# Two 128-unit chunks per turn of the first matmul, in the order whole, tiled, tiled, whole

## The chip, the cores and the metric

The kernel runs on one core of one Trainium2 chip. The time is that of the device, in microseconds (us), from one launch. Three runs of the kernel before gave 829.6, 832.7 and 833.99 us, median 832.7 us. The profile comes from one more execution, of 831.74 us. Its span, from the first to the last recorded event, is 829.9 us. Engines are named as in the profile: PE is TensorE running matmuls, PEld is TensorE loading weights, DVE is VectorE, ACT is ScalarE, POOL is GpSimd and SP is SyncE.

## The reference

A short causal convolution over tokens is followed by a two-layer network with a gated activation. Eight sequences of 4096 tokens have 192 channels each; the hidden layer has 2048 units.

```python
# convolution: 7 taps, softmax-normalised weights, one set for each of 8 heads of 24 channels
w = softmax(weight, axis=-1)                   # (8, 7)
conv[b, s, h, g] = sum_k w[h, k] * x_pad[b, s + k, h, g]
# network, on 8 * 4096 = 32768 tokens of 192 channels
h = conv @ w_in                                # (32768, 192) @ (192, 2048)
g = h * (1.0 / (1.0 + np.exp(-beta * h)))
out = g @ w_out                                # (32768, 2048) @ (2048, 192)
```

## The kernel before

The work is cut into 32 stages (`N_ST`). One stage holds 512 tokens (`TOK`) of each of two sequences, called halves `h` here; so a stage has 1024 tokens. Channels lie on the partitions. Channels 0 to 127 of both halves stand in `ct[:, 0, :]` and `ct[:, 1, :]`. The other 64 channels of the two halves share one slice: `ct[0:64, 2, :]` belongs to half 0 and `ct[64:128, 2, :]` to half 1. The weights `w_in_s` have the same split: `[:, 0, :]` for the first 128 channels and `[:, 1, :]` for the last 64, held twice, on rows 0 to 63 and again on rows 64 to 127.

**First matmul (`hidden`).** The 2048 hidden units are cut into 16 chunks (`NF`) of 128. For each chunk there are four matmuls of 512 columns into a tile `ph` of two PSUM banks, one bank for each half. Two take the first 128 channels, and so all 128 rows of the array (line 218, called *whole* below, W). Two take the last 64 channels, one on rows 0 to 63 and the other on rows 64 to 127 (line 221, called *tiled*, T). Then ScalarE applies the activation from `ph` into `g` (line 224). Each matmul has its own weight load. There are three `ph` buffers.

**Second matmul (`output`).** For each block of 128 tokens, sixteen matmuls add up over the hidden units, with `g` as the weights and 192 columns of `w_out_s` (line 239, called O below). A part is half a block, eight matmuls. Every fourth part is followed by a VectorE copy of `po` (line 247), and every eighth part by a store from SyncE's queue.

**Order.** The schedule is written by hand and each engine runs its instructions in program order. In the main loop a stage has 16 turns `u`. In turn `u` the kernel issues chunk `u` of the first matmul of stage `s`, part `u` of the second matmul of stage `s - 1`, and one VectorE operation of the convolution of stage `s + 1` (14 in all, lines 195, 197 and 206). Stage 0 has no second matmul. Its VectorE also scales the weights: `prep_w_in` (line 170) ahead of turns 0, 4, 8 and 12, and `prep_w_out` (line 177) in every turn. After stage 31 a last pass has only the 16 parts of the second matmul.

On TensorE a turn of stages 1 to 31 is therefore: two W, two T, eight O.

Of the kernel before, what the change touches and what calls it, by code (L numbers as in the profile page):

```python
# [8 lines left out]
FP32 = mybir.dt.float32  # L9
BF16 = mybir.dt.bfloat16  # L10
AF = mybir.ActivationFunctionType
# [4 lines left out]
def kernel(  # L16
# [15 lines left out]
    nc = tc.nc  # L32
# [6 lines left out]
    DB = D - DA  # L39
    TOK = 512  # L40
# [4 lines left out]
    N_ST = (B // 2) * CHUNKS  # L45
# [18 lines left out]
    psum_h = ctx.enter_context(  # L64
        tc.tile_pool(name="psum_h", bufs=3, space=bass.MemoryType.PSUM)
    )
# [9 lines left out]
    def cast(s):  # L76
        p, c = divmod(s, CHUNKS)
        r0 = HALO if c == 0 else 0
        t0 = c * TOK - HALO + r0
        t1 = (c + 1) * TOK  # L80
        xd = xd_pool.tile([HALO + TOK, 3, DA], BF16, name="xd")
        nc.gpsimd.dma_start(out=xd[r0:, 0:2, :], in_=x_v[p, t0:t1, :, 0:DA])  # L82
        nc.gpsimd.dma_start(  # L83
            out=xd[r0:, 2, :].rearrange("t (h d) -> t h d", h=2),
            in_=x_v[p, t0:t1, :, DA:D],
        )
        xds[s] = xd

    def xpose(s):
        r0 = HALO if s % CHUNKS == 0 else 0  # L90
        xd = xds.pop(s)
        xt = xt_pool.tile([128, 3, HALO + TOK], BF16, name="xt")
        if r0:
            nc.vector.memset(xt[:, :, 0:HALO], 0.0)
        nc.sync.dma_start_transpose(  # L95
            xt[:, :, r0:], xd[r0:, :, :].rearrange("t c d -> t (c d)")
        )
        xts[s] = xt
# [61 lines left out]
    beta = consts.tile([128, NF], FP32)  # L160
# [4 lines left out]
    w_in_s = consts.tile([128, 2, F], BF16)  # L165

    def prep_w_in(i):
        cols = slice(i * FW, (i + 1) * FW)
        for j in range(2):
            nc.vector.tensor_scalar_mul(  # L170
                w_in_s[:, j, cols], w_in_raw[i][:, j, :], w_last[:, j : j + 1]
            )
# [3 lines left out]
    def prep_w_out(c):  # L176
        nc.vector.tensor_scalar_mul(  # L177
            w_out_s[:, c, :], w_out_raw[:, c, :], beta_r[:, c : c + 1]
        )
# [4 lines left out]
    def conv_ops(s):  # L184
        xt = xts.pop(s)
        ct = ct_pool.tile([128, 3, TOK], BF16, name="ct")
        cts[s] = ct
        ops = []
        for j, cs in ((0, slice(0, 2)), (1, slice(2, 3))):

            def tap(k, j=j, cs=cs):
                src = xt[:, cs, HALO - PAD + k : HALO - PAD + k + TOK]
                dst = ct[:, cs, :]
                if k == 0:
                    nc.vector.tensor_scalar_mul(dst, src, cw[:, j, 0:1])  # L195
                elif k < K - 1:
                    nc.vector.scalar_tensor_tensor(  # L197
                        out=dst,
                        in0=src,
                        scalar=cw[:, j, k : k + 1],  # L200
                        in1=dst,
                        op0=ALU.mult,
                        op1=ALU.add,
                    )
                else:
                    nc.vector.tensor_tensor(dst, src, dst, ALU.add)  # L206

            ops += [lambda k=k, tap=tap: tap(k) for k in range(K)]
        return ops

    gs = {}

    def hidden(s, fc):
        ct, g = cts[s], gs[s]
        ph = psum_h.tile([128, 2, TOK], FP32, name="ph")
        w = w_in_s[:, :, fc * 128 : (fc + 1) * 128]
        for h in range(2):
            nc.tensor.matmul(ph[:, h, :], w[:, 0, :], ct[:, h, :], start=True, stop=False)  # L218
        for h in range(2):
            rows = slice(h * DB, (h + 1) * DB)  # L220
            nc.tensor.matmul(  # L221
                ph[:, h, :], w[rows, 1, :], ct[rows, 2, :], start=False, stop=True
            )
        nc.scalar.activation(g[:, fc, :, :], ph, AF.Silu, scale=beta[:, fc : fc + 1])  # L224

    pos, osbs = {}, {}

    def output(s, part):

        blk, half = divmod(part, 2)  # L230
        h, q = divmod(blk, N_BLK)
        g = gs[s]
        if part % 4 == 0:
            pos[s] = psum_o.tile([128, 2, D], FP32, name="po")
        if part % 8 == 0:
            osbs[s] = osb_pool.tile([128, N_BLK, D], FP32, name="osb")
        po, osb = pos[s], osbs[s]
        for fc in range(half * NF // 2, (half + 1) * NF // 2):
            nc.tensor.matmul(  # L239
                po[:, q % 2, :],  # L240
                g[:, fc, h, q * BLK : (q + 1) * BLK],
                w_out_s[:, fc, :],
                start=(fc == 0),
                stop=(fc == NF - 1),
            )
        if part % 4 == 3:
            nc.vector.tensor_copy(osb[:, q - 1 : q + 1, :], po)  # L247
        if part % 8 == 7:
            p, c = divmod(s, CHUNKS)
            nc.sync.dma_start(out=out_v[h, p, c], in_=osb)  # L250
# [4 lines left out]
    for s in range(N_ST + 1):  # L255
        if s < N_ST:
            gs[s] = g_pool.tile([128, NF, 2, TOK], BF16, name="g")
        ops = conv_ops(s + 1) if s + 1 < N_ST else []
        for u in range(NF):
            if s == 0 and u % (NF // NW) == 0:  # L260
                prep_w_in(u // (NF // NW))
            if s < N_ST:
                hidden(s, u)
            if s > 0:
                output(s - 1, u)
            if u < len(ops):
                ops[u]()
            if s == 0:
                prep_w_out(u)
            if u == 0 and s + 3 < N_ST:  # L270
                cast(s + 3)
            if u == 1 and s + 2 < N_ST:
                xpose(s + 2)
# [30 lines left out]
```

## Time and profile before

| what | us |
|---|---|
| three runs, median (lowest, highest) | 832.7 (829.6, 833.99) |
| the profiled execution, its own time | 831.74 |
| its span | 829.9 |
| PE busy | 784.3 |
| PEld busy | 445.7 |
| ACT busy | 572.7 |
| DVE busy | 462.8 |
| from the first O (61.67) to the last turn's O (814.07) | 752.40 |

Times in the span count from its start. A row of the timeline has the start, the length, the engine, the line, the operation, the output and inputs and how many instructions were merged; a square bracket at the end holds the idle time of the engine ahead of it and what ended it. Matmuls are pipelined and the end of one is modelled: two that overlap in the rows run one behind the other on the array. So matmuls are compared by their starts, not by their lengths.

### The profile page before, as it was taken

What the parts mean: (1) busy time and instruction counts of PE and PEld (TensorE: products, weight loads), DVE (VectorE), ACT (ScalarE), POOL (GpSimd) and SP (SyncE); (2) the same over time, 40 slices, a digit from 0 to 9 for tenths busy, and PEclk for the clock granted to TensorE, in tenths of its full rate; (3) what the DMA queues carried; (4) which work ended last, traced back from release to release, by engine and by line L of the source; (5) the groups of instructions that cost most, each with busy time, mean ns of one, the idle gap of its engine ahead of it and who ended that gap; (6) DMA issues with size and microseconds to landing.
All of it is one profiled execution on the core that took longest, in us unless ns stands there. A gap on an engine that the chain in (4) does not pass through costs nothing.

```text
span 829.9 us, 13854 instructions
## 1 busy us (share of the span) xinstructions
PE 784.3 (95%) x6145; PEld 445.7 (54%) x6145; DVE 462.8 (56%) x613; ACT 572.7 (69%) x516; POOL 82.5 (10%) x70
## 2 busy tenths in 40 slices
PE   0279999999999999999999999999999999999997
PEld 0015555555555555555555555555555555555556
DVE  2696665555656556565555656555565665555601
ACT  1267777777777777777777777777777777777772
POOL 8389800000000000000000000000000000000000
PEclk9989999999999999999999999999999999999999
DMA  9999991210322221122222112222201322220111
GB/s 143 222 169 179 182 120 41 58 53 25 59 58 46 53 58 43 35 59 58 39 58 59 36 42 59 58 39 58 59 28 51 59 59 39 58 54 25 39 39 59
DMA packets 157341, 55.60 MB, mean 67 GB/s; under 512 B 121425, under 2 KB 156257, under 8 KB 157281
## 3 DMA queue, kind: packets, MB, share of 16 engines
q1 hardware_dynamic: 88592, 41.77, 22.1%
q0 software_dynamic: 68352, 12.93, 18.9%
q8 instruction: 48, 0.79, 0.4%
q10 hardware_dynamic: 337, 0.02, 0.0%
q14 instruction: 12, 0.10, 0.0%
HBM read 29.54 MB, written 38.09 MB: 81 GB/s over the span
## 4 chain that ended last, share of the span: by engine, by line
PE 93%; DMA 4%; DVE 2%; SPq 1%; issue 0%; POOL 0%; POOLq 0%
PE po L239 47%; PE ph L218 26%; PE ph L221 20%; DMA xt<-xd 2%; DMA w_in_raw_107<-in_moe_w_in_dram 1%; DVE ct L197 1%; DMA xd<-in_x_dram 1%; DVE w_out_s L177 1%; DVE w_in_s L170 0%; SPq L95 0%; SPq L133 0%; SPq L131 0%; DVE ct L195 0%; DVE ct L206 0%; SPq L136 0%
## 5 line engine op out<-in xcount | busy, mean ns | idle before, releaser
L224 ACT ACTIVATE g<-ph,beta 128x1024 bf16<-128x1024 f32 x512 | 569.6, 1114 | 233.6 <-PE ph L221 233.6
L239 PE MATMUL po<-w_out_s,g 128*128 128x192 bf16 x4096 | 424.0, 247 | 0.0
L239 PEld LDWEIGHTS <-g 128*128 128x128 bf16 x4096 | 312.4, 98 | 112.2 <-issue 112.2
L218 PE MATMUL ph<-ct,w_in_s 128*128 128x512 bf16 x1024 | 308.2, 383 | 31.1 <-DVE w_in_s L170 31.1
L197 DVE SCALAR_TENSOR_TENSOR ct<-xt,cw,ct 128x1024 bf16<-128x1024 bf16 (+1 forms) x320 | 325.1, 1016 | 8.8
L247 DVE COPY osb<-po 128x384 f32<-128x384 f32 x128 | 71.4, 557 | 329.0 <-PE po L239 329.0
L221 PE MATMUL ph<-ct,w_in_s 64*128 64x512 bf16 x1024 | 201.7, 391 | 0.8 <-DVE w_in_s L170 0.8
L221 PEld LDWEIGHTS <-w_in_s 64*128 64x128 bf16 x1024 | 49.3, 93 | 221.3 <-issue 217.8
L218 PEld LDWEIGHTS <-w_in_s 128*128 128x128 bf16 x1024 | 91.3, 98 | 36.8 <-DVE w_in_s L170 32.3
L82 POOL DMA_DIRECT2D xd<-in_x_dram x32 | 42.6, 1330 | 12.4 <-DMA xd<-in_x_dram 11.6
L83 POOL DMA_DIRECT2D xd<-in_x_dram x32 | 42.5, 1327 | 8.3 <-DMA xd<-in_x_dram 7.9
L206 DVE TENSOR_TENSOR ct<-xt,ct 128x1024 bf16<-128x1024 bf16 x64 | 35.7, 557 | 2.1
L195 DVE TENSOR_SCALAR ct<-xt,cw 128x1024 bf16<-128x1024 bf16 x64 | 27.6, 431 | 14.1 <-DMA xt<-xd 13.3
L177 DVE TENSOR_SCALAR w_out_s<-w_out_raw,beta_r 128x192 bf16<-128x192 f32 x16 | 8.9, 568 | 0.0
L159 PE MATMUL po<-ident,beta_q 16*128 16x16 f32 x1 | 0.3, 254 | 9.2 <-DMA beta_q<-in_moe_beta_dram 9.2
L146 ACT ACT_TABLE_LOAD x1 | 1.3, 1283 | 6.1 <-DMA cw<-in_weight_dram 6.1
L159 PEld LDWEIGHTS po<-ident,beta_q 16*128 16x128 f32 x1 | 0.2, 176 | 9.1 <-issue 9.1
L144 DVE TENSOR_REDUCE nmax<-cw 128x2 f32<-128x14 f32 x1 | 0.2, 168 | 7.7 <-DMA cw<-in_weight_dram 7.7
L224 ACT ACT_TABLE_LOAD x1 | 1.3, 1283 | 1.5 <-DVE beta L161 1.5
L170 DVE TENSOR_SCALAR w_in_s<-w_in_raw_115,w_last 128x512 bf16<-128x512 f32 x2 | 1.5, 800 | 0.0
L146 ACT ACTIVATE cw<-cw,nmax 128x7 f32<-128x7 f32 x2 | 0.5, 294 | 1.4 <-DVE nmax L144 1.4
L170 DVE TENSOR_SCALAR w_in_s<-w_in_raw_111,w_last 128x512 bf16<-128x512 f32 x2 | 1.5, 774 | 0.0
(16 smaller groups left out, 4.7 us busy)
## 6 DMA issues: line engine op xcount, KB each, us to landing
out_dram<-osb SPq DMA_DIRECT2D x64, 384.0 KB, 3.0
xd<-in_x_dram POOLq DMA_DIRECT2D x28, 264.0 KB, 10.1
xd<-in_x_dram POOLq DMA_DIRECT2D x28, 132.0 KB, 10.2
w_out_raw<-in_moe_w_out_dram SPq DMA_DIRECT2D x1, 1536.0 KB, 12.8
xd<-in_x_dram POOLq DMA_DIRECT2D x4, 256.0 KB, 9.1
xd<-in_x_dram POOLq DMA_DIRECT2D x4, 128.0 KB, 8.7
xt<-xd SPq DMA_TRANSPOSE x32, 4.6
w_in_raw_103<-in_moe_w_in_dram SPq DMA_DIRECT2D x1, 256.0 KB
```

Source lines behind the costliest of these rows:

```text
L82: nc.gpsimd.dma_start(out=xd[r0:, 0:2, :], in_=x_v[p, t0:t1, :, 0:DA])
L83: nc.gpsimd.dma_start(out=xd[r0:, 2, :].rearrange("t (h d) -> t h d", h=2), in_=x_v[p, t0:t1, :, DA:D],)
L170: nc.vector.tensor_scalar_mul(w_in_s[:, j, cols], w_in_raw[i][:, j, :], w_last[:, j : j + 1])
L177: nc.vector.tensor_scalar_mul(w_out_s[:, c, :], w_out_raw[:, c, :], beta_r[:, c : c + 1])
L195: nc.vector.tensor_scalar_mul(dst, src, cw[:, j, 0:1])
L197: nc.vector.scalar_tensor_tensor(out=dst, in0=src, scalar=cw[:, j, k : k + 1], in1=dst, op0=ALU.mult, op1=ALU.add,)
L206: nc.vector.tensor_tensor(dst, src, dst, ALU.add)
L218: nc.tensor.matmul(ph[:, h, :], w[:, 0, :], ct[:, h, :], start=True, stop=False)
L221: nc.tensor.matmul(ph[:, h, :], w[rows, 1, :], ct[rows, 2, :], start=False, stop=True)
L224: nc.scalar.activation(g[:, fc, :, :], ph, AF.Silu, scale=beta[:, fc : fc + 1])
L239: nc.tensor.matmul(po[:, q % 2, :], g[:, fc, h, q * BLK : (q + 1) * BLK], w_out_s[:, fc, :], start=(fc == 0), stop=(fc == NF - 1),)
L247: nc.vector.tensor_copy(osb[:, q - 1 : q + 1, :], po)
```

## The change

`hidden` now takes two chunks at once and is called in every second turn `u`. Two `ph` tiles are taken together. The eight matmuls of the two chunks stand in the order W W of the first chunk, T T of the first, T T of the second, W W of the second. In the second chunk the tiled matmuls now start the accumulation and the whole ones end it. The two activations follow. Everything else in the loop stays, so the outputs of parts `u` and `u + 1`, sixteen matmuls, now stand one behind the other on TensorE, and a *turn* of the changed kernel is: two W, two T, two T, two W, sixteen O. The numbers of matmuls, weight loads and activations are the same.

```diff
-    def hidden(s, fc):
+    def hidden(s, fc0):
         ct, g = cts[s], gs[s]
-        ph = psum_h.tile([128, 2, TOK], FP32, name="ph")
-        w = w_in_s[:, :, fc * 128 : (fc + 1) * 128]
-        for h in range(2):
-            nc.tensor.matmul(ph[:, h, :], w[:, 0, :], ct[:, h, :], start=True, stop=False)
-        for h in range(2):
-            rows = slice(h * DB, (h + 1) * DB)
-            nc.tensor.matmul(
-                ph[:, h, :], w[rows, 1, :], ct[rows, 2, :], start=False, stop=True
-            )
-        nc.scalar.activation(g[:, fc, :, :], ph, AF.Silu, scale=beta[:, fc : fc + 1])
+        phs = [psum_h.tile([128, 2, TOK], FP32, name="ph") for _ in range(2)]
+        ws = [w_in_s[:, :, f * 128 : (f + 1) * 128] for f in (fc0, fc0 + 1)]
+
+        def whole(i, start):
+            for h in range(2):
+                nc.tensor.matmul(
+                    phs[i][:, h, :], ws[i][:, 0, :], ct[:, h, :], start=start, stop=not start
+                )
+
+        def tiled(i, start):
+            for h in range(2):
+                rows = slice(h * DB, (h + 1) * DB)
+                nc.tensor.matmul(
+                    phs[i][:, h, :], ws[i][rows, 1, :], ct[rows, 2, :], start=start, stop=not start
+                )
+
+        whole(0, True)
+        tiled(0, False)
+        tiled(1, True)
+        whole(1, False)
+        for i in range(2):
+            fc = fc0 + i
+            nc.scalar.activation(
+                g[:, fc, :, :], phs[i], AF.Silu, scale=beta[:, fc : fc + 1]
+            )
...
-            if s < N_ST:
+            if s < N_ST and u % 2 == 0:
                 hidden(s, u)
```

Before, TensorE's queue in the middle of a stage has, for one chunk (`ph_1017`), W, W, T, T, and then the outputs. Each row names the line, the instruction, and its output and inputs with their buffer numbers; LDWEIGHTS is the weight load ahead of each matmul. L218 is W, L221 is T, L239 is O.

```order
L218 LDWEIGHTS w_in_s_149
L218 MATMUL ph_1017<-ct_565,w_in_s_149 128x512 [waits Activation_49]
L218 LDWEIGHTS w_in_s_149
L218 MATMUL ph_1017<-ct_565,w_in_s_149 128x512
L221 LDWEIGHTS w_in_s_149
L221 MATMUL ph_1017<-ct_565,w_in_s_149 128x512
L221 LDWEIGHTS w_in_s_149
L221 MATMUL ph_1017<-ct_565,w_in_s_149 128x512
L239 LDWEIGHTS g_564
L239 MATMUL po_1023<-w_out_s_150,g_564 128x192 [waits DVE_49]
```

The outputs stand right behind the two T, and the only wait for ScalarE in the chunk is at its first W. In the changed kernel, at the same place of TensorE's queue, L221 is W and L228 is T (the line numbers have moved); `ph_1017` is the first chunk of the turn and `ph_1018` the second.

```order
L228 LDWEIGHTS w_in_s_149
L228 MATMUL ph_1017<-ct_565,w_in_s_149 128x512
L228 LDWEIGHTS w_in_s_149
L228 MATMUL ph_1017<-ct_565,w_in_s_149 128x512
L228 LDWEIGHTS w_in_s_149
L228 MATMUL ph_1018<-ct_565,w_in_s_149 128x512 [waits Activation_49]
L228 LDWEIGHTS w_in_s_149
L228 MATMUL ph_1018<-ct_565,w_in_s_149 128x512
L221 LDWEIGHTS w_in_s_149
L221 MATMUL ph_1018<-ct_565,w_in_s_149 128x512
```

Four T now stand together, the second chunk's W follow them, and there is a second wait for ScalarE, in the middle of the turn, at the second chunk's first T. The end of the turn on the same engine, where L255 is O:

```order
L221 LDWEIGHTS w_in_s_149
L221 MATMUL ph_1018<-ct_565,w_in_s_149 128x512
L255 LDWEIGHTS g_564
L255 MATMUL po_1029<-w_out_s_150,g_564 128x192 [waits DVE_49]
L255 LDWEIGHTS g_564
L255 MATMUL po_1029<-w_out_s_150,g_564 128x192
```

The outputs now follow a W, not a T.

## The prediction

> **What bounds the kernel.** I read the page's busy shares first, then the chain of work that ended last, then the stretch in which the 31 equal stages lie, and last the timeline of one chunk.
>
> ```profile
> span 829.9 us, 13854 instructions
> PE 784.3 (95%) x6145; PEld 445.7 (54%) x6145; DVE 462.8 (56%) x613; ACT 572.7 (69%) x516; POOL 82.5 (10%) x70
> PEclk9989999999999999999999999999999999999999
> ...
> PE 93%; DMA 4%; DVE 2%; SPq 1%; issue 0%; POOL 0%; POOLq 0%
> ```
>
> TensorE is 93% of the chain, with its clock granted in full from the second tenth of the span on, and no other engine is near its limit. What counts is therefore the distance between matmul starts. The view by stretches gives the stages 1 to 31 in one row; its columns are length, busy time of PE, PEld, DVE, ACT and POOL with counts, the clock, the DMA share and GB/s.
>
> ```profile
> 61.66:814.06 752.40, 752.40 (x5942) 430.53 (x5940) 422.17 (x545) 551.80 (x496) 39.27 (x31) 1.00 0.32 58
> ```
>
> The timeline has the first and the last O of that stretch:
>
> ```profile
> 61.67 0.83 PE L239 MATMUL po<-w_out_s,g 128*128 128x192 bf16 x8
> ...
> 814.07 11.39 PE L239 MATMUL po<-w_out_s,g 128*128 128x192 bf16 x136
> ```
>
> From the O of the first chunk of stage 1 to the O of the last chunk of stage 31 are 495 chunks: 752.40 / 495 = 1.520 us for one chunk, at clock 1.00. PE counts as busy all of that time, so no wait of another engine shows in it. Now one chunk, from the timeline:
>
> ```profile
> 403.66 0.61 PEld L239 LDWEIGHTS <-g 128*128 128x128 bf16 x8 [0.23 <-issue]
> 403.67 0.83 PE L239 MATMUL po<-w_out_s,g 128*128 128x192 bf16 x8
> ...
> 404.25 0.18 PEld L218 LDWEIGHTS <-w_in_s 128*128 128x128 bf16 x2
> 404.34 0.59 PE L218 MATMUL ph<-ct,w_in_s 128*128 128x512 bf16 x2
> 404.86 0.10 PEld L221 LDWEIGHTS <-w_in_s 64*128 64x128 bf16 x2 [0.42 <-issue]
> 404.86 0.39 PE L221 MATMUL ph<-ct,w_in_s 64*128 64x512 bf16 x2
> 405.18 0.61 PEld L239 LDWEIGHTS <-g 128*128 128x128 bf16 x8 [0.23 <-issue]
> 405.19 0.83 PE L239 MATMUL po<-w_out_s,g 128*128 128x192 bf16 x8
> 405.30 1.11 ACT L224 ACTIVATE g<-ph,beta 128x1024 bf16<-128x1024 f32 x1 [0.41 <-PE ph L221]
> 405.77 0.18 PEld L218 LDWEIGHTS <-w_in_s 128*128 128x128 bf16 x2
> 405.86 0.59 PE L218 MATMUL ph<-ct,w_in_s 128*128 128x512 bf16 x2
> ```
>
> And the groups of the same stretch (62 to 814 us), with their mean lengths in ns and the idle time ahead of them:
>
> ```profile
> L239 PE MATMUL po<-w_out_s,g 128*128 128x192 bf16 x3959 | 412.5, 247 | 0.0
> L239 PEld LDWEIGHTS <-g 128*128 128x128 bf16 x3956 | 301.0, 98 | 111.8 <-issue 111.8
> L218 PE MATMUL ph<-ct,w_in_s 128*128 128x512 bf16 x990 | 294.4, 379 | 0.0
> L221 PE MATMUL ph<-ct,w_in_s 64*128 64x512 bf16 x990 | 193.2, 387 | 0.0
> L218 PEld LDWEIGHTS <-w_in_s 128*128 128x128 bf16 x990 | 89.2, 98 | 0.0
> L221 PEld LDWEIGHTS <-w_in_s 64*128 64x128 bf16 x990 | 47.6, 93 | 209.9 <-issue 209.9
> ```
>
> The steps of a chunk follow from these:
> - W to W: a pair takes 294.4 / 495 = 0.595 us from its first start to its last end; less one length of 0.379 leaves 0.216 us between the two starts. That is what 512 columns take.
> - T beside T: 193.2 / 495 = 0.390 us for a pair, less 0.387, leaves 0.003 us. The two tiled matmuls run side by side, on two halves of the rows.
> - O to O, undisturbed: in the final run of 136, (11.39 - 0.247) / 135 = 0.0825 us.
> - O block: 405.19 to 405.86, 0.670 us for eight; 8 x 0.0825 is 0.660, so 0.010 is lost at its start.
> - What is left of 1.520, after 0.670 and 0.216, is 0.634 us: second W to first T (404.34 + 0.216 to 404.86, about 0.31) and T to O (404.86 to 405.19, about 0.32). Were both only 512 columns long, they would take 0.432. So **0.202 us** go at the two crossings, about 0.096 going into the tiled form and 0.106 coming out of it, and 0.010 more in the first O.
>
> The load rows show why. A W's load has no idle time ahead of it (0.0 in 990): it goes in while the matmul ahead still runs. The load of the T pair comes 209.9 / 495 = 0.42 us after the load ahead of it has ended, although it was next in the queue, and starts with its own matmul (404.86 both). After T the O's load waits 111.8 / 495 = 0.23 us in the same way. At each crossing between 128*128 and 64*128 the loads are not taken ahead.
>
> **The change part by part.** *Crossings.* A chunk before has two crossings, so two chunks have four. The changed turn W W T T T T W W O x16 has two: W to T once, T to W once. Step by step, by starts: W0 to W0 0.216; W0 to T0 0.312; T0 to T1 0.216 (chosen, see below); T1 to W1 0.322; W1 to W1 0.216; W1 to O 0.216; sixteen O at 0.0825, 1.320. The sum is 2.818 us a turn, against 2 x 1.520 = 3.040. The saving is **0.222 us a turn**: 0.202 for the two crossings gone and 2 x 0.010 in the first O, because now a W, whose 0.216 is longer than a load of 0.098, lies between the crossing and the O. If the 0.010 came back once in the turn, the saving would be 0.212; that is 2.5 us in all, which I keep for the range. There are 31 stages x 8 = 248 turns: 248 x 0.222 = **55.1 us**.
>
> *T0 to T1, the one step that the trace does not show.* Nowhere in the kernel before does a T follow a T on the same rows. The nearest rows bound it: W to W, the same form behind the same form, takes 0.216 and hides its loads, so the extra is 0; a crossing costs 0.106 at most. At the crossing's price the turn is 0.096 to 0.106 longer, 24 to 26 us in all. Below zero the row gives nothing: 0.216 is the column time of each W as well. I take 0, since the row nearest in kind is the unchanged form, where the loads have 0.0 idle although they go to all the rows on which the matmul ahead runs.
>
> [...]
>
> *The second wait for ScalarE.* Two `ph` tiles of three are now taken in a turn. The second T pair reuses the tile of the first chunk of the turn before, and waits for its activation; behind it in the queue are T1, W1 and sixteen O. An activation takes 1.11 us and starts 0.44 after its T (404.86 to 405.30). In the new turn T0 starts at 0.528, so the first activation runs from 0.97 to 2.08 and the second to about 3.2. T1 of the next turn starts at 2.818 + 0.744 = 3.56, 1.5 us after the tile is free; the first W of the turn after that, at 5.64, needs the second activation, at 3.2. ScalarE has 2.23 us of work in 2.82. So the wait costs nothing; even if the first activation were held until W1 ended, about 0.75 later, it would be done at 2.8. That cover would be gone only if a turn fell towards 2.23 us.
>
> *VectorE.* Its copies and taps keep their order. The last of a stage:
>
> ```profile
> 395.42 0.56 DVE L247 COPY osb<-po 128x384 f32<-128x384 f32 x1 [2.90 <-PE po L239]
> 395.89 1.53 DVE L197 SCALAR_TENSOR_TENSOR ct<-xt,cw,ct 128x512 bf16<-128x512 bf16 x2
> 397.45 0.42 DVE L206 TENSOR_TENSOR ct<-xt,ct 128x512 bf16<-128x512 bf16 x1
> ```
>
> The next stage begins on PE with
>
> ```profile
> 401.30 0.59 PE L218 MATMUL ph<-ct,w_in_s 128*128 128x512 bf16 x2
> ```
>
> The tile `ct` is finished at 397.87, 3.43 us ahead of the W that needs it. In the new order the copy is released by the last O of the sixth turn, with two turns, 5.64 us, to go; the chain behind it is 2.45 us long, so some 3 us are left. The queues of SyncE and GpSimd keep their rows; a stage of 22.5 instead of 24.3 us leaves their transfers, at a DMA share of 0.32, room.
>
> *Stage 0.* It has no O and is paced by VectorE, which prepares the weights; the last pair of scalings ends at 56.41:
>
> ```profile
> 54.89 1.52 DVE L170 TENSOR_SCALAR w_in_s<-w_in_raw_115,w_last 128x512 bf16<-128x512 f32 x2
> ```
>
> Only the four chunks behind it gain, two turns of 0.2 at most, and part of it meets ScalarE's 1.11 a chunk. I take 0.2, bounds 0 and 0.5. The last pass of O is unchanged.
>
> *Sum.* 829.9 - 55.1 - 0.2 = 774.6 us of span. The profiled execution took 831.74, 1.84 over its span: 776.4. The median of the runs shown, 832.7, is 1.0 above the profiled one; I say **777**.
>
> **The rivals.**
> *1. T to T is no better than a crossing.* The 0.1 us would then belong to every tiled pair whose rows are in use, not to the change of form. A turn is 2.818 + 0.096 to 0.106 = 2.91 to 2.92 us, the saving 0.116 to 0.126 a turn or 29 to 31 us: **801 to 803 us**. For it: the tiled loads have no instance in the trace in which they are taken ahead. Against it: all whole loads are. This is also the way in which the change would fail to do what it says: the order is changed, but the cost stays with the tiled matmuls.
> *2. Partly hidden.* T1's loads wait for T0's last column but not for the crossing's full time; 93 ns is one load, and at a crossing the matmul starts with its load. Between 0 and 0.096, say 0.05: 12 us more, **789 us**.
> *3. Slower: the four tiled matmuls no longer run in pairs.* If T1 of half 0 waits for T0 on its rows with its load, and T1 of half 1 only issues behind that with a wait of its own, each costs 0.312: T0 to T1 to T1 to the next, 0.096 + 0.312 = 0.408 more a turn, against 0.222 saved. Net 0.186 x 248 = 46 us on the profiled 831.7: **878 us**. It decides from 0.222 us lost in the four T on. Against it: the pair starts 0.003 us apart even when both loads have to wait at a crossing. For it: only that pairs behind pairs are not in the trace.
>
> **How the numbers follow.** Forecast 0.68 (774 to 780); rival 1 0.18; rival 2 0.09; rival 3 0.03; 0.02 for a gain that is lost in a wait that I do not see, ending near 832. The range reaches from 773 (the full saving on a run as low as the lowest shown, 829.6 - 55.1 - 0.5 = 774, and 1 for the spread of runs) to 803, the end of rival 1; rival 3 and the last 0.02 are left out. A measurement of this kernel can tell about 0.5% from no change; faster by more than that holds 0.95, within it 0.02, slower 0.03.
>
> **What would show it.** The stretch of 31 stages shrinks by 55 us to about 697; the two T pairs of a turn start 0.216 apart; the loads of the second pair have no idle ahead of them, so the idle time ahead of tiled loads is about halved, and that ahead of O loads is gone and stands at the second W pair. ScalarE's idle per turn falls to about 0.6. Wrong would be: T pairs 0.31 apart (rival 1), a wait of PE for ScalarE or VectorE inside the stages, tiled matmuls that start apart by more than a few ns (rival 3), or W to O longer than 0.216.

## The result and the profile after

| what | before | after |
|---|---|---|
| median of the runs compared, us | 831.15 (828.9 to 833.99, 4 runs) | 776.42 (775.1 to 778.94, 4 runs) |
| ratio to before, 95% interval | | 0.9343 (0.9302 to 0.9385) |
| the profiled execution, us | 831.74 | 777.03 |
| its span, us | 829.9 | 775.2 |
| two chunks of the stages 1 to 31, us | 2 x 1.520 | 2.827 |

The changed kernel is 6.6% faster. In its lines L221 is W, L228 is T, L255 is O and L238 the activation. The page's first part and its chain, as shown of before:

```profile
span 775.2 us, 13754 instructions
PE 714.3 (92%) x6045; PEld 446.5 (58%) x6145; DVE 461.7 (60%) x613; ACT 545.6 (70%) x516; POOL 82.5 (11%) x70
...
PE 90%; DMA 4%; issue 2%; DVE 2%; SPq 1%; POOL 0%; POOLq 0%
```

TensorE is still the bound. All 6145 weight loads are in the trace, but only 6045 of the matmuls: 100 records of W are missing, and the page counts what they leave open as "issue" or as less busy time. The steps are therefore read only where both neighbours are there. The first W of the second turn and the last turn's first W, from the timeline:

```profile
61.92 0.59 PE L221 MATMUL ph<-ct,w_in_s 128*128 128x512 bf16 x2
...
757.28 0.38 PE L221 MATMUL ph<-ct,w_in_s 128*128 128x512 bf16 x1
```

They are 246 turns apart: 695.36 / 246 = 2.827 us a turn. One turn of the timeline:

```profile
403.87 0.18 PEld L221 LDWEIGHTS <-w_in_s 128*128 128x128 bf16 x2
403.95 0.38 PE L221 MATMUL ph<-ct,w_in_s 128*128 128x512 bf16 x1
...
404.48 0.11 PEld L228 LDWEIGHTS <-w_in_s 64*128 64x128 bf16 x4 [0.42 <-issue]
404.48 0.60 PE L228 MATMUL ph<-ct,w_in_s 64*128 64x512 bf16 x4
...
404.91 2.12 ACT L238 ACTIVATE g<-ph,beta 128x1024 bf16<-128x1024 f32 x2 [0.71 <-PE ph L228]
405.01 0.11 PEld L221 LDWEIGHTS <-w_in_s 128*128 128x128 bf16 x2 [0.42 <-issue]
405.02 0.60 PE L221 MATMUL ph<-ct,w_in_s 128*128 128x512 bf16 x2
405.25 1.47 PEld L255 LDWEIGHTS <-g 128*128 128x128 bf16 x16
405.46 1.48 PE L255 MATMUL po<-w_out_s,g 128*128 128x192 bf16 x16
406.70 0.18 PEld L221 LDWEIGHTS <-w_in_s 128*128 128x128 bf16 x2
406.78 0.59 PE L221 MATMUL ph<-ct,w_in_s 128*128 128x512 bf16 x2
```

The four loads of the two T pairs stand in one row, 0.11 us long: the second pair's loads go in as soon as the first pair has started. A window that cuts off the first pair shows where the second begins:

```profile
404.71 0.38 PE L228 MATMUL ph<-ct,w_in_s 64*128 64x512 bf16 x2
```

So T0 to T1 is 404.48 to 404.71, 0.23 us, against the 0.216 forecast and the 0.31 of a crossing. W to T is 0.53 from the first W, of which 0.216 are the step from W to W, so 0.31; T1 to W1 0.31 (404.71 to 405.02); from there to O 0.44 for two steps, W1 to W1 and W1 to O; sixteen O 1.32. The idle time ahead of the loads, 62 to 760 us, against before's 209.9 ahead of T and 111.8 ahead of O:

```profile
L255 PEld LDWEIGHTS <-g 128*128 128x128 bf16 x3952 | 333.6, 98 | 58.5
...
L221 PEld LDWEIGHTS <-w_in_s 128*128 128x128 bf16 x987 | 72.4, 97 | 104.8 <-issue 104.8
...
L228 PEld LDWEIGHTS <-w_in_s 64*128 64x128 bf16 x988 | 28.0, 94 | 104.6 <-issue 104.6
```

Ahead of T it has halved. Ahead of O no load waits for "issue" any more; the 58.5 left, 0.24 a turn, lie between loads that went in early: the first O's load, at 405.25, went in during the last W, whose 0.216 is longer than a load of 0.098, and the next one, at 405.46, during the first O. The second crossing now stands at the W, 104.8.

### The profile page after: what moved, and what is told of

Read it like the earlier page. It is cut to its first block, busy times and chain, and to the rows that moved or that the text cites. A ratio compares the mean times of both kernels' runs of the same rounds, so it can differ in the third digit from the quotient of the medians.

```text
span 775.2 us, 13754 instructions
## 1 busy us (share of the span) xinstructions
PE 714.3 (92%) x6045; PEld 446.5 (58%) x6145; DVE 461.7 (60%) x613; ACT 545.6 (70%) x516; POOL 82.5 (11%) x70
## 4 chain that ended last, share of the span: by engine, by line
PE 90%; DMA 4%; issue 2%; DVE 2%; SPq 1%; POOL 0%; POOLq 0%
PE po L255 44%; PE ph L221 29%; PE ph L228 18%; DMA xt<-xd 2%; DVE ct L197 1%; DMA w_in_raw_107<-in_moe_w_in_dram 1%; DMA xd<-in_x_dram 1%; DVE w_out_s L177 0%; DVE w_in_s L170 0%; SPq L95 0%; SPq L133 0%; SPq L131 0%; DVE ct L195 0%; DVE ct L206 0%; SPq L136 0%
## 5 line engine op out<-in xcount | busy, mean ns | idle before, releaser
L238 ACT ACTIVATE g<-ph,beta 128x1024 bf16<-128x1024 f32 x512 | 542.6, 1110 | 205.7 <-PE ph L228 204.9
L255 PEld LDWEIGHTS <-g 128*128 128x128 bf16 x4096 | 345.5, 98 | 58.7
L255 PE MATMUL po<-w_out_s,g 128*128 128x192 bf16 x4096 | 378.5, 246 | 0.0
L221 PE MATMUL ph<-ct,w_in_s 128*128 128x512 bf16 x924 | 287.7, 385 | 38.7 <-DVE w_in_s L170 31.0
L228 PE MATMUL ph<-ct,w_in_s 64*128 64x512 bf16 x1024 | 156.5, 384 | 8.0 <-DVE w_in_s L170 0.6
L221 PEld LDWEIGHTS <-w_in_s 128*128 128x128 bf16 x1024 | 75.4, 98 | 144.6 <-issue 111.5
L228 PEld LDWEIGHTS <-w_in_s 64*128 64x128 bf16 x1024 | 29.3, 94 | 111.0 <-issue 107.9
L82 POOL DMA_DIRECT2D xd<-in_x_dram x32 | 41.4, 1295 | 12.1 <-DMA xd<-in_x_dram 11.1
L83 POOL DMA_DIRECT2D xd<-in_x_dram x32 | 41.4, 1294 | 10.2 <-DMA xd<-in_x_dram 10.2
```

The lines of the kernel that those rows point to most:

```text
L83: nc.gpsimd.dma_start(out=xd[r0:, 2, :].rearrange("t (h d) -> t h d", h=2), in_=x_v[p, t0:t1, :, DA:D],)
L221: nc.tensor.matmul(phs[i][:, h, :], ws[i][:, 0, :], ct[:, h, :], start=start, stop=not start)
L228: nc.tensor.matmul(phs[i][:, h, :], ws[i][rows, 1, :], ct[rows, 2, :], start=start, stop=not start)
L238: nc.scalar.activation(g[:, fc, :, :], phs[i], AF.Silu, scale=beta[:, fc : fc + 1])
L255: nc.tensor.matmul(po[:, q % 2, :], g[:, fc, h, q * BLK : (q + 1) * BLK], w_out_s[:, fc, :], start=(fc == 0), stop=(fc == NF - 1),)
```

## The experiments

**E1: two chunks per turn, but W T W T.** All else of the change is kept, the four crossings per two chunks are back.

```diff
         whole(0, True)
         tiled(0, False)
-        tiled(1, True)
-        whole(1, False)
+        whole(1, True)
+        tiled(1, False)
```

> Two chunks and sixteen O per turn as in the changed kernel, but the order is W T W T, so a turn has four crossings between the whole and the tiled form, as two turns of before have. Theory (all of the gain is the two crossings taken out, about 0.106 us each with the 0.010 in the step behind it): a turn of 2 x 1.520 = 3.040 us, no gain in the 31 stages, 829 to 833 us in all. Rival (the gain comes from two chunks per turn, from the longer run of O or from fewer changes between the two matmuls): a turn of about 2.83 us, 776 us.

Measured: 830.39 us against 830.46 of before, ratio 0.9996 (0.9982 to 1.001). The timeline of two turns' starts, PE alone:

```profile
400.80 0.39 PE L228 MATMUL ph<-ct,w_in_s 64*128 64x512 bf16 x2
401.12 0.61 PE L221 MATMUL ph<-ct,w_in_s 128*128 128x512 bf16 x2
401.66 0.39 PE L228 MATMUL ph<-ct,w_in_s 64*128 64x512 bf16 x2
401.98 1.50 PE L255 MATMUL po<-w_out_s,g 128*128 128x192 bf16 x16
403.31 0.59 PE L221 MATMUL ph<-ct,w_in_s 128*128 128x512 bf16 x2
403.84 0.39 PE L228 MATMUL ph<-ct,w_in_s 64*128 64x512 bf16 x2
```

From T to T of the next turn, 400.80 to 403.84, are 3.04 us. Two chunks in a turn and sixteen O in a row are worth nothing by themselves: with everything else of the change kept, all of the gain goes with the order of T and W.

**E2: W W T T.** Two crossings, at other places.

```diff
         whole(0, True)
+        whole(1, True)
         tiled(0, False)
-        tiled(1, True)
-        whole(1, False)
+        tiled(1, False)
```

> Order W W T T, then sixteen O: two crossings per turn, as in the changed kernel, but the tiled matmuls end both chunks and stand next to O. Theory (only the number of crossings counts, not where they are): a turn of 4 W at 0.216 with the crossing 0.312 as the last, T to T 0.226, T to O 0.312, sixteen O 1.320 + 0.010 = 2.83 us, as the changed kernel's 2.827; 775 to 779 us. Rival (W as the last of the turn matters, since loads of O behind a T are slower or the activation of the first chunk, now 0.43 us later, meets a wait): 2.9 us a turn or more, 790 us or more.

Measured: 777.6 us, ratio 0.9368 (0.935 to 0.9385). A turn from T to T:

```profile
401.14 0.61 PE L228 MATMUL ph<-ct,w_in_s 64*128 64x512 bf16 x4
401.68 1.49 PE L255 MATMUL po<-w_out_s,g 128*128 128x192 bf16 x16
403.01 1.03 PE L221 MATMUL ph<-ct,w_in_s 128*128 128x512 bf16 x3
403.97 0.60 PE L228 MATMUL ph<-ct,w_in_s 64*128 64x512 bf16 x4
```

401.14 to 403.97 is 2.83 us, as in the changed kernel. Between these two orders it does not matter where the crossings stand, only how many there are.

**E3: no tiled form.** The 64 channels of a half go through all 128 rows, with zeros as the weights of the other half's rows.

```diff
...
-            rows = slice(h * DB, (h + 1) * DB)
             nc.tensor.matmul(
-                ph[:, h, :], w[rows, 1, :], ct[rows, 2, :], start=False, stop=True
+                ph[:, h, :],
+                w_pad[:, h, fc * 128 : (fc + 1) * 128],
+                ct[:, 2, :],
+                start=False,
+                stop=True,
             )
```

> The kernel before with no tiled form at all: the last 64 channels of each half go through the whole array, with the weights of the other 64 rows set to zero (so one half's matmul runs over the other half's rows and adds nothing). A chunk has four W-like matmuls one behind the other instead of two W and a T pair, and no crossing; VectorE prepares one more weight slice in stage 0. Theory (a crossing costs 0.106 because the form changes): a chunk of 4 x 0.216 + 8 x 0.0825 = 1.524 us, no idle ahead of any load, so the 31 stages stay within 2 us of before; 831 to 838 us with the extra preparation. Rival (the loads waited because of the weights' slice, the input slice or the change from one matmul to the next, not because of the form): the crossing's 0.2 us stay beside the longer column time, 1.73 us a chunk, 930 us or more.

Measured: 837.38 us in one run, before 831.09. Of the 6 us more, 4.1 are ahead of the first O, at 65.77 instead of 61.67, where VectorE prepares the padded weights. (Between profiled executions of E4, E7 and E8, whose stage 0 is the same, this start also moves by 4 us, so the 4.1 need not all be the preparation; the stages are compared by their steps.) The timeline, PE alone in the rows chosen:

```profile
400.04 0.59 PE L225 MATMUL ph<-ct,w_in_s 128*128 128x512 bf16 x2
...
400.47 0.59 PE L227 MATMUL ph<-ct,w_pad 128*128 128x512 bf16 x2
...
400.90 0.82 PE L249 MATMUL po<-w_out_s,g 128*128 128x192 bf16 x8
...
401.56 0.59 PE L225 MATMUL ph<-ct,w_in_s 128*128 128x512 bf16 x2
```

Four matmuls from 400.04 to 400.90 take 0.86 us, 4 x 0.215, and the chunk 1.52. The same input slice, with the same weights in a tile padded with zeros, costs no extra time once the form stays the same; and in the changed kernel T behind T reads the old slice of the weights and pays no crossing (0.23 us from T0 to T1). So it is the change of form that the crossing's cost belongs to. In the kernel before the tiled pair saved one step of 0.216 and paid 0.212 for its two crossings: it gained nothing.

**E4: groups of three chunks.** W T T T W W, in groups of 3, 3, 3, 3, 2, 2 a stage.

```diff
...
         whole(0, True)
         tiled(0, False)
-        tiled(1, True)
-        whole(1, False)
+        for i in range(1, n):
+            tiled(i, True)
+        for i in range(1, n):
+            whole(i, False)
...
-            if s < N_ST and u % 2 == 0:
-                hidden(s, u)
+            if s == 0 and u % 2 == 0:
+                hidden(s, u, 2)
+            if 0 < s < N_ST and u in GROUPS:
+                hidden(s, u, GROUPS[u])
```

> In stages 1 to 31 the sixteen chunks go in groups of 3, 3, 3, 3, 2, 2 (W T T T W W), each followed by as many parts of O; stage 0 stays in pairs. Six groups have 12 crossings per stage where eight turns have 16. Theory: a stage of 16 x 1.308 + 6 x 0.212 = 22.20 us instead of 8 x 2.827 = 22.61, 31 x 0.42 = 13 us less than the changed kernel: 762 to 765 us, about 0.918 of before. Rival (all three ph tiles are taken in a group, so the third T pair or the next W waits for ScalarE): PE shows waits for the activation and the time stays at 770 us or more.

Measured: 764.0 us, ratio 0.9207 (0.9183 to 0.9231), which lies clear of the changed kernel's interval. The groups of loads and the activation, 62 to 740 us:

```profile
L239 ACT ACTIVATE g<-ph,beta 128x1024 bf16<-128x1024 f32 x490 | 512.6, 1112 | 166.7 <-PE ph L227 166.7
...
L220 PEld LDWEIGHTS <-w_in_s 128*128 128x128 bf16 x978 | 77.8, 97 | 106.7 <-issue 77.6
L227 PEld LDWEIGHTS <-w_in_s 64*128 64x128 bf16 x978 | 32.8, 94 | 92.1 <-issue 77.6
```

No load waits for an activation, so the rival is out; ScalarE still waits for TensorE. The waits for "issue" fell from 104.6 to 77.6, by about the quarter by which the crossings became fewer.

**E5: two `ph` buffers.** `bufs=3` of `psum_h` becomes `bufs=2`.

> The changed kernel with two ph buffers instead of three: each chunk then waits for the activation of the chunk two back. Theory (the wait for ScalarE is covered with room): in a turn both activations end about 3.08 us after its first W, the next turn's second T pair, which then needs the second activation, comes at 2.83 + 0.75 = 3.58, so 0.5 us are left and the 31 stages keep 2.827 a turn; only stage 0, which has no O, may lose up to 3 us: 775 to 780 us. Rival (the slack of the activation is smaller than worked out): waits of PE for ScalarE in every turn, 0.1 us or more each, 800 us or more.

Measured: 776.98 us, ratio 0.9359 (0.9344 to 0.9374). A turn:

```profile
401.53 0.60 PE L228 MATMUL ph<-ct,w_in_s 64*128 64x512 bf16 x4
401.96 2.12 ACT L238 ACTIVATE g<-ph,beta 128x1024 bf16<-128x1024 f32 x2 [0.65 <-PE ph L228]
...
404.36 0.60 PE L228 MATMUL ph<-ct,w_in_s 64*128 64x512 bf16 x4
```

Both activations end at 404.08, ahead even of the next turn's first T, and the turn is 2.83 us. In the stages with O the new wait for ScalarE costs nothing, with room to spare, as worked out; in stage 0, which has no O, TensorE waits for ScalarE three times, 1.1 us in all.

**E6: four crossings per chunk.** The kernel before, with the T pair cut into two pairs of 256 columns, one in the middle of the eight O.

```diff
+        def tiled(c):
+            cols = slice(c * TOK // 2, (c + 1) * TOK // 2)
+            for h in range(2):
+                rows = slice(h * DB, (h + 1) * DB)
+                nc.tensor.matmul(
+                    ph[:, h, cols], w[rows, 1, :], ct[rows, 2, cols], start=False, stop=c == 1
+                )
...
+            if fc % (NF // 2) == NF // 4 - 1:
+                between()
```

> The kernel before with the tiled pair cut into two pairs of 256 columns, the second one in the middle of the eight O: W W T' O O O O T' O O O O, four crossings per chunk instead of two, the same columns in all, two weight loads more. Theory (each crossing costs 0.096 and 0.010 in the step behind it, whatever stands there): 1.520 + 2 x 0.106 = 1.732 us a chunk, 496 x 0.212 = 105 us more, about 936 us. Rival (the cost belongs to a chunk's tiled work as a whole, or grows with the length of the matmul that has to run out): half of that or less, 880 us at most.

Measured: 936.75 us in one run. The timeline, PE alone in the rows chosen:

```profile
400.52 0.28 PE L224 MATMUL ph<-ct,w_in_s 64*128 64x256 bf16 x2
...
400.73 0.51 PE L247 MATMUL po<-w_out_s,g 128*128 128x192 bf16 x4
...
402.25 0.28 PE L224 MATMUL ph<-ct,w_in_s 64*128 64x256 bf16 x2
402.47 0.51 PE L247 MATMUL po<-w_out_s,g 128*128 128x192 bf16 x4
```

A chunk is 1.73 us. T of 256 columns to O takes 0.21, 0.108 for its columns and 0.10 for the crossing: the price is the same behind a matmul of half the length. A chunk now pays for four crossings, and no part of the price follows the columns, so the rival is out. This and E3 are single runs, but the differences that they rest on, 0.2 us a chunk or 100 us in all, are far beyond the spread of the others.

**E7: groups of three across the ends of the stages.** The groups of E4 run on through all stages (chunk number `c`), with three `g` buffers.

```diff
...
-            if 0 < s < N_ST and u in GROUPS:
-                hidden(s, u, GROUPS[u])
+            if 0 < s < N_ST and (c - NF) % 3 == 0:
+                hidden(c, min(3, N_ST * NF - c))
```

> Groups of three chunks run on across the ends of the stages (165 groups of three and one chunk alone, three g buffers instead of two). Theory: 166 turns with two crossings instead of 31 x 6 = 186, 20 x 0.212 = 4.2 us less than the groups of 3, 3, 3, 3, 2, 2: 758 to 761 us. Rival (the next stage's first chunk now comes up to two chunks earlier, and the convolution, whose last VectorE operation ends about 3 us ahead of the stage, is not ready): waits of PE for VectorE at the ends of the stages eat it, 763 us or more.

Measured: 765.64 us, ratio 0.9222 (0.9183 to 0.926), no better than E4. The timeline at one stage end, and below it the waits:

```profile
501.75 0.60 PE L231 MATMUL ph<-ct,w_in_s 64*128 64x512 bf16 x4
502.62 0.39 PE L231 MATMUL ph<-ct,w_in_s 64*128 64x512 bf16 x2 [0.27 <-DVE ct L206]
```

```profile
PEld L231 <- DVE ct L206: 7.6, 10, 0.8
...
PE ph L231 <- DVE ct L206: 2.7, 10, 0.3
```

The rival was right. The third T pair of a group is the next stage's first chunk, and it starts 502.62 - 501.75 = 0.87 us after the first pair instead of the 0.44 of two undisturbed steps (0.226 and 0.216). Ten stage ends lose about 0.43 each, 4.3 us, which is the 4.2 us of gain expected.

**E8: the convolution earlier.** E7 with VectorE's 14 operations in the first ten parts.

```diff
-            if u < len(ops):
-                ops[u]()
+            if s == 0:
+                if u < len(ops):
+                    ops[u]()
+            else:
+                for op in ops[u * 14 // 10 : (u + 1) * 14 // 10]:
+                    op()
```

> Groups of three across the ends of the stages, with VectorE's 14 operations for the next stage issued in the first ten parts of a stage instead of the first fourteen, ahead of the last copies. Theory (in the run across the stages TensorE waited 0.42 us for the end of the convolution at ten of the stage ends, 4.2 us in all, which is what the 20 turns less should have brought): no wait of PE for VectorE, from the first O to the last T 4.2 us less than there, 680.9 us instead of 685.05, and 758 to 762 us in all. Rival (the copies of the output are held up behind the operations and TensorE waits for them instead): waits of PE for the copy, 763 us or more.

Measured: 760.42 us (758.96 to 764.01), ratio 0.9162 (0.9134 to 0.919). The first O, the last T and the last row of O, and below them the last row of O of E4:

```profile
64.63 2.14 PE L259 MATMUL po<-w_out_s,g 128*128 128x192 bf16 x24
...
745.27 0.39 PE L231 MATMUL ph<-ct,w_in_s 64*128 64x512 bf16 x2
745.60 11.39 PE L259 MATMUL po<-w_out_s,g 128*128 128x192 bf16 x136
```

```profile
744.94 12.04 PE L258 MATMUL po<-w_out_s,g 128*128 128x192 bf16 x144
```

The first O and the last T are 680.64 us apart, 680.9 expected, and no wait for VectorE is left. Its interval overlaps that of E4, so by the times alone the two are not told apart; both beat the changed kernel. The traces do tell them apart. The last 128 O of each begin at 746.26 (16 O of 0.0825 us behind 744.94 in E4, 8 behind 745.60 here). From the first O, at 60.42 in E4 and at 64.63 here, that is 685.84 and 681.63 us: 4.2 less, the gain that 20 turns fewer should bring.

## Why the prediction was right, and where its sizes were off

777 was forecast, 776.42 measured, and the mechanism is the one named: crossings taken out. That the sum is this close is in part luck, since two terms were off with opposite signs.

- **Crossings.** E1 gives the gain back in full with nothing but the order of four matmuls, E2 keeps it with another order of two crossings, E6 adds the price twice, 105.7 us against 105 worked out. At full clock, 0.096 at a crossing and 0.010 in the step behind it hold in all of them.
- **T0 to T1, the unseen step.** Forecast 0.216, measured 0.23. No load waits for T0 to end, so rivals 1, 2 and 3 fall: T1's loads go to T0's rows and have still ended within 0.11 us of T0's start. The 0.010 over the forecast is not T's own, since a W behind a crossing has it as well (W1 to W1 and W1 to O take 0.44 together, where 2 x 0.216 is 0.432). E3 agrees from the other side: where all matmuls have one form, four of them take 0.86, with no crossing among them.
- **The turn.** Forecast 2.818, measured 2.827. The term that was mis-sized is the 0.010 of the first O. I had seen it as belonging to O and gone when a W follows the crossing; the steps show that the step behind any crossing is 0.010 longer: T0 to T1 behind W to T, W to W behind T to W. The 0.322 that I took for T1 to W1 had such a 0.010 in it, because in the kernel before T to O stands right behind the other crossing; here this step is 0.311. So two steps are 0.010 longer than forecast and one is 0.011 shorter, and 0.2133 a turn were saved, not 0.222: 248 x 0.2133 = 52.9 us instead of 55.1. The prediction had kept this case, 0.212, for its range.
- **Stage 0.** Forecast 0.2, bounds 0 and 0.5. The span became 54.7 shorter, so about 1.8 us are left for it, more than the bound. They lie ahead of the first O, which begins at 60.60 instead of 61.67, though one chunk more (some 0.85 us) now stands ahead of it. Two things make them up. VectorE ends its last scaling of the weights at 55.36 (53.84 and 1.52 in the row below), where before it was 56.41. That is 1.05 us, and it is not shown to come from the change: in E4, E7 and E8, which have the same stage 0, this scaling ends at 53.95, 55.96 and 58.16 in the profiled executions. The other part is TensorE's way from there to the first O, 5.24 us instead of 5.26 with a chunk more, a gain of some 0.87. This part is steady, 6.47 in each of E4, E7 and E8. The order of the chunks is in it, since E1, with as many chunks ahead of its first O, takes 6.09 at a granted clock of 0.73; the clock may be too, as 0.68 was granted on this way before and 0.75 after. How much belongs to each stays open. The two errors, 2.2 us too much for the turns and 1.6 too little for stage 0, nearly cancel.
- **The waits.** No wait of TensorE for ScalarE or VectorE in the stages, as forecast; E5 shows that even one `ph` buffer less would do. ScalarE's idle time is 0.71 a turn (174.2 us in 247), where 0.6 was forecast. The slack of some 3 us that I gave the convolution was real but not large: E7 used it up.

The scaling in stage 0 of the changed kernel:

```profile
53.84 1.52 DVE L170 TENSOR_SCALAR w_in_s<-w_in_raw_115,w_last 128x512 bf16<-128x512 f32 x2
```

## What to carry to other kernels

Count the changes between the whole array and row tiles in TensorE's program order, and price them: here one costs about 0.106 us, half the 0.216 of a 512-column matmul, so that a single tiled pair between whole matmuls, as in this kernel before, saves nothing over zero-padded weights. Put tiled matmuls of several accumulations together, which needs as many open PSUM tiles as accumulations; each can begin or end with its tiled part. When such a group is made to cross a stage, look at what the next stage's first input then still waits for.

## What the runs showed that was not expected

The crossing's price follows neither the columns of the matmul ahead (0.10 behind 256 as behind 512) nor, as a sum, the clock. In stage 0 of the changed kernel the clock was granted by half in this window (the columns are as in the stretches before the change; the clock follows POOL's count):

```profile
55.42:57.63 2.21, 2.21 (x7) 0.56 (x8) 2.21 (x4) 1.29 (x2) 2.21 (x2) 0.50 2.07 172
```

There the timeline has, for T0 T0 T1 T1 and the W behind them, and with the first pair cut off for T1 T1:

```profile
55.41 1.04 PE L228 MATMUL ph<-ct,w_in_s 64*128 64x512 bf16 x4 [0.60 <-DVE w_in_s L170]
...
56.38 1.80 PE L221 MATMUL ph<-ct,w_in_s 128*128 128x512 bf16 x4
```

```profile
55.81 0.64 PE L228 MATMUL ph<-ct,w_in_s 64*128 64x512 bf16 x2
```

T0 to W is 0.97 us. Two steps at half the clock are, by estimate, about 2 x 2 x 0.216 = 0.864 (a W to W at half clock, 45.88 to 46.30, is 0.42), so some 0.11 (0.13 with that step) are left for the crossing, where the full clock gives 0.54 - 0.432 = 0.11 as well. The same step from 44.51 to 45.48, at half clock too, is again 0.97. But the parts are not the same. At half clock T0 to T1 is 0.40, shorter than a step of 0.432 and not 0.010 longer, and T1 to W is 0.57, so about 0.14 over a step instead of 0.096. What the array does in this time was not tried. It is not simply the length of a load that nothing hides: the matmul behind a crossing starts with its load (404.48 both in the turn shown), not behind it.
